# Pooled attention and a GELU layer on one core: k of the later batches turned by a transposing DMA, and four smaller edits

## The chip, the cores and the metric

The kernel runs on one core of one Trainium2 chip. The metric is the device time in microseconds of one execution, as the median of several runs. A profiled execution gives a span (first to last instruction that the hardware profiler saw) and a trace of every engine: TensorE (PE, its weight loads as PEld), VectorE (DVE), ScalarE (ACT), GpSimd (POOL) and SyncE (SP). SP, ACT and POOL also issue DMAs.

## The reference

For each of 8 batches and 8 heads, k and v (576 rows of 64) are averaged over groups of 8 rows, which leaves 72 pooled rows. Then softmax attention of the 576 rows of q against them, and a two-layer network on all 4608 rows:

```python
k_p = k.reshape(B, H, Sp, pool, D).mean(axis=3)       # B=8 H=8 S=576 D=64 pool=8 Sp=72
v_p = v.reshape(B, H, Sp, pool, D).mean(axis=3)
attn = softmax(q @ k_p.T / sqrt(D))
x = (attn @ v_p).transpose(0, 2, 1, 3).reshape(4608, 512)
h = x @ w_in                                           # 512 x 2048
out = gelu_tanh(h) @ w_out                             # 2048 x 512
```

## The kernel before

**Groups.** The order of all instructions is written out by hand. Batch 0's attention is a start of its own. Then nine groups of 512 rows of the network follow (`for g in range(NG)`). A group has two halves. In p1, 64 matmuls of 512 columns (`p1_mm`, 16 tiles `fo` of four steps `ko`) make h, and ACT applies gelu to each tile into `gT`. In p2, 64 matmuls of 512 columns (`p2_mm`, four row blocks `r` of 16 steps) make the output; `store` copies a block from PSUM to one of six buffers `osb` on VectorE, and SP sends it out in four DMAs. Between the p2 matmuls, at the hand-set places `pos`, lies the attention of the next batch `nb = g + 1`: `qk` (scores of two heads), `expo` (exponential on ACT), `av` (attention times v, with the denominator in the unused half of the columns), `norm` and `mult`.

**k and v.** `load_k` brings k of a batch to `kt`, four pooled rows of 2 KB to a partition, head after head, as 128 partitions of 8 KB and a rest of 64 partitions in a fifth slot; the lower 64 partitions of that slot take v's last eight pooled rows of every head. `k_steps` are three additions on VectorE that halve the eight summands each time and leave `kp`. `trans_k_mm` (L173) turns `kp` on TensorE in five transposes, and `trans_k_copy` copies the result from PSUM into two tiles `kT`, six copies each (L183 to L194). Each of the two has 64 of its 128 rows filled and the others zero. For a head in the upper half of the heads, the pooled rows are placed so that rows 64 to 127 come first and eight rows stand at 0 to 7; `pool_rows` says how many rows are used (72 or 128), and `vp`, `vz` and `ones` are laid out alike. `v_steps` adds v's main rows (64 of each head) into `vp`; `v_moves` moves the last eight by two DMAs on SP.

**q.** Batches 0 and 1 are turned on TensorE (L203). From batch 2 on, `load_q` (on POOL, with a cast to bf16) brings q to `qb`, and `trans_q_dma` (L223) turns it by a transposing DMA on SP, which waits for the load.

**Loads ahead.** `load_next` issues, for batch g + 2: the q load on POOL, the q transpose on SP, a tiny copy on POOL (`gate`, L453) that holds POOL until the transpose has landed, and then the k and v loads on POOL. In groups 1 to 5 it stands at the start of the group, in group 0 behind p1. Since POOL has nothing else to do, the q load of a batch is issued right behind the v loads of the batch before.

**What lies beside p1.** The dictionary `plan` says behind which gelu the additions, transposes and copies are emitted: in groups from 1 on, k's additions behind tiles 2 and 3, v's behind 7 and 8, and the five transposes of k behind 9.

**The start.** Batch 0's k and v are loaded first, by SP and ACT. POOL then loads q of batch 0, w_in in two parts, k of batch 1, q of batch 1 and w_out in four parts. v of batch 1 is loaded by SP once VectorE has reached a one-element memset of its tile (L421), which stands after the first `mult0`. In group 0 p2 takes w_out quarter by quarter.

**The end.** The last row block of the last group is split by columns into 384 and 128; each part is copied and stored in four DMAs, two on SP and two on ACT.

Of the kernel before, what the change touches and what calls it, by code (L numbers as in the profile page):

```python
# [8 lines left out]
F32 = mybir.dt.float32  # L9
# [9 lines left out]
def kernel(  # L19
# [9 lines left out]
    nc = tc.nc  # L29
# [23 lines left out]
    opool = ctx.enter_context(tc.tile_pool(name="op", bufs=6))  # L53
# [11 lines left out]
    kts = [consts.tile([128, KR + 1, 512], F32, name=f"kt{i}") for i in range(2)]  # L65

    def load_k(b, engs):
        rows = k[b].rearrange("h (j l) d -> (h j) (l d)", l=8)
        main = rows[0:128 * KR].rearrange("(p r) c -> p r c", r=KR)
        n = KR // len(engs)  # L70
        for i, eng in enumerate(engs):
            eng.dma_start(out=kts[b % 2][:, i * n:(i + 1) * n], in_=main[:, i * n:(i + 1) * n])
        engs[0].dma_start(out=kts[b % 2][64:128, KR], in_=rows[128 * KR:])
        rows = v[b].rearrange("h (j l) d -> j h (l d)", l=8)
        for i in range(2):
            engs[-1].dma_start(out=kts[b % 2][32 * i:32 * i + 32, KR], in_=rows[64:, 4 * i:4 * i + 4])  # L76
# [41 lines left out]
    kTs = [[consts.tile([128, H, 128], BF16, name=f"kT{i}{e}") for e in range(2)] for i in range(2)]  # L118
    kps = [consts.tile([128, KR + 2, D], BF16, name=f"kp{i}") for i in range(2)]

    vps = [consts.tile([128, H, 2, D], BF16, name=f"vp{i}") for i in range(2)]

    vz = consts.tile([128, H, 2, D], BF16, name="vz")
    ones = consts.tile([128, 2, 3, D], BF16, name="ones")
# [6 lines left out]
    for half, j0, j1 in ((0, 0, 128), (1, 0, 8), (1, 64, 128)):  # L131
        nc.vector.memset(ones[j0:j1, half, 1], 8.0)
# [4 lines left out]
    def add(o, a, b):  # L137
        nc.vector.tensor_tensor(out=o, in0=a, in1=b, op=ALU.add)  # L138
# [8 lines left out]

    def v_moves(b):

        for i in range(2):  # L150
            nc.sync.dma_start(out=vps[b % 2][64 - 64 * i:72 - 64 * i, 4 * i:4 * i + 4, 0],
                              in_=kps[b % 2][32 * i:32 * i + 32, KR])

    def v_steps(b):
        t = vts[b % 2]
        w = (vps[b % 2] if b else vz)[:, :, 0]

        def main():
            for i in range(2):
                p = slice(64 * i, 64 * i + 64)  # L160
                add(w[p, 4 * i:4 * i + 4], t[p, :, 0:64], t[p, :, 64:128])

        return [lambda: add(t[:, :, 0:256], t[:, :, 0:256], t[:, :, 256:512]),
                lambda: add(t[:, :, 0:128], t[:, :, 0:128], t[:, :, 128:256]), main]
# [10 lines left out]
    def trans_k_copy(b, e, bank, lower=True, upper=True):  # L175


        tp = half_bank(bank)[0:D, 0:(KR + 1) * 128].rearrange("p (r c) -> p r c", c=128)
        o = kTs[b % 2][e][e * 64:(e + 1) * 64]
        copy = nc.vector.tensor_copy  # L180

        def heads(h0, h1, c0, j0, j1):
            copy(out=o[:, h0:h1, c0:c0 + (j1 - j0) * KR].rearrange("p h (j r) -> p h j r", r=KR),  # L183
                 in_=tp[:, 0:KR, h0 * KH:h1 * KH].rearrange("p r (h j) -> p h j r", j=KH)[:, :, j0:j1])

        if lower:
            heads(0, 4, 0, 0, KH)
        if upper:
            heads(4, H - 1, 64, 0, 16)
            heads(4, H - 1, 0, 16, KH)  # L190
            copy(out=o[:, H - 1, 64:72].rearrange("p (j r) -> p j r", r=KR),
                 in_=tp[:, 0:KR, (H - 1) * KH:128].rearrange("p r j -> p j r"))
            copy(out=o[:, H - 1, 72:128], in_=tp[:, KR, 64:120])
            copy(out=o[:, H - 1, 0:8], in_=tp[:, KR, 120:128])  # L194
# [36 lines left out]
    def pool_rows(pr):  # L231
        return Sp if pr < PR // 2 else 128

    def qk(b, c, pr, bank):
        for e in range(2):
            h = 2 * pr + e
            n = pool_rows(pr)
            nc.tensor.matmul(out=PS[:n, bank + e, :CH].rearrange("j (t p) -> j t p", p=32),  # L238
                             lhsT=kTs[b % 2][c][:, h, :n],
                             rhs=qTs[b][:, h // 4, :, h % 4 * 32:h % 4 * 32 + 32],  # L240
                             start=True, stop=True)

    def expo(b, c, pr, bank):
        n = pool_rows(pr)
        e = ep.tile([128, 2, CH], BF16, name="e", bufs=8)
        nc.scalar.activation(out=e[:n], in_=PS[:n, bank:bank + 2, :CH], func=ACT.Exp, scale=1.0 / 64.0)  # L246
        es[b, c, pr] = e
# [6 lines left out]
    def av(b, c, pr, bank):  # L254


        e = es.pop((b, c, pr))
        n = pool_rows(pr)
        for x in range(2):
            nc.tensor.matmul(out=PS[:, bank + x, :CH], lhsT=window(vps[b % 2][:n], 2 * pr + x),  # L260
                             rhs=e[:n, x, :], start=True, stop=True)
# [20 lines left out]
    def den0(c, pr, bank):  # L282
        for x in range(2):
            e = es[0, c, pr + x]
            n = pool_rows(pr)
            for y in range(2):
                one = ones[:n, pr // 2].rearrange("j a d -> j (a d)")[:, 64 - 64 * y:192 - 64 * y]
                nc.tensor.matmul(out=PS[:, bank + x, :CH], lhsT=one, rhs=e[:n, y, :],
                                 start=(y == 0), stop=(y == 1))
# [8 lines left out]
    def av0(c, pr, bank):  # L298
        for x in range(2):
            e = es.pop((0, c, pr + x))  # L300
            n = pool_rows(pr)
            for y in range(2):
                nc.tensor.matmul(out=PS[:, bank + x, :CH], lhsT=window(vz[:n], 2 * (pr + x) + y),
                                 rhs=e[:n, y, :], start=(y == 0), stop=(y == 1))
# [22 lines left out]
    def o_bank(g, r):  # L327
        return 1 - x_bank(g) if r % 2 == 0 else x_bank(g)
# [3 lines left out]
    def p1_mm(g, fo, ko, c0=0, c1=GROUP):  # L332
        r0 = g * GROUP
        q, j = divmod(fo % 8, 4)
        nc.tensor.matmul(out=PS[:, h_bank(g, fo), c0:c1], lhsT=w_in_b[fo // 8][:, ko, q * 512 + j:(q + 1) * 512:4],  # L335
                         rhs=xT[:, ko, r0 + c0:r0 + c1], start=(ko == 0), stop=(ko == KO - 1))

    def gelu(g, fo):
        if g not in gTs:
            gTs[g] = gpool.tile([128, FO, GROUP], BF16, name="gT")  # L340
        nc.scalar.activation(out=gTs[g][:, fo, :], in_=PS[:, h_bank(g, fo), :], func=ACT.Gelu_apprx_tanh)  # L341
# [5 lines left out]
    osbs = {}  # L347

    def store(g, r, bank, c0=0, c1=DM):
        if (g, r) not in osbs:  # L350
            osbs[g, r] = opool.tile([128, DM], F32, name="osb")
        osb = osbs[g, r]
        nc.vector.tensor_copy(out=osb[:, c0:c1], in_=PS[:, bank, c0:c1])  # L353

        for n in range(4):
            b, col = divmod(g * GROUP + r * 128 + n * 32, S)
            rows = out[b * S:(b + 1) * S].rearrange("(p t e) d -> e t p d", t=TP, e=2)
            eng = nc.scalar if c1 - c0 < DM and n % 2 else nc.sync
            eng.dma_start(out=rows[col // CH, col % CH // 32, :, c0:c1], in_=osb[n * 32:(n + 1) * 32, c0:c1])
# [30 lines left out]
    for h in range(H):  # L390
        i = h // 4
        nc.tensor.matmul(out=PS[64 - 64 * i:72 - 64 * i, 7, h * D:(h + 1) * D],
                         lhsT=identb[0:64, 32 * i + h % 4:32 * i + 32:4], rhs=kps[0][0:64, KR],
                         start=True, stop=True)
# [3 lines left out]
    for i in range(2):  # L398
        p = slice(64 - 64 * i, 72 - 64 * i)
        nc.vector.tensor_copy(out=vz[p, 4 * i:4 * i + 4, 0],  # L400
                              in_=PS[p, 7, 256 * i:256 * i + 256].rearrange("p (h d) -> p h d", d=D))
# [18 lines left out]

    nc.vector.memset(vts[1][:, 0, 0:1], 0.0)  # L421
    load_v(1, [nc.sync])
# [12 lines left out]
    nc.vector.memset(kTs[1][1], 0.0)  # L435
    for w in vps:
        nc.vector.memset(w, 8.0)
        nc.vector.memset(w[0:64, H // 2:], 0.0)
        nc.vector.memset(w[0:8, H // 2:], 8.0)
# [5 lines left out]
    for g in range(NG):  # L445
# [3 lines left out]
        def load_next():  # L449

            load_q(g + 2)
            trans_q_dma(g + 2)
            nc.gpsimd.tensor_copy(out=gate, in_=qTs[g + 2][0:1, 1, TP - 1, 0:2])  # L453
            load_k(g + 2, [nc.gpsimd])
            load_v(g + 2, [nc.gpsimd])

        if 0 < g and g + 2 < B:
            load_next()
# [3 lines left out]
        if nb is not None:  # L462
            kk = k_steps(nb)
# [3 lines left out]
            if g:  # L467
# [64 lines left out]
    for c0, c1, bank in ((0, 384, o_bank(g, 3)), (384, DM, 4)):  # L532
        for fo in range(FO):
            p2_mm(g, 3, fo, bank, c0, c1)
        store(g, 3, bank, c0, c1)
# [30 lines left out]
```

The softmax here doesn't subtract the row's maximum and nothing guards it: scores larger than these inputs give would overflow.

## Time and profile before

| | |
|---|---|
| median of 3 runs | 307.75 us (306.88 to 308.21) |
| profiled execution | 307.9 us, span 306.1 us |
| TensorE busy | 296.8 us, 97% of the span |
| ScalarE, VectorE, GpSimd busy | 219.0, 150.5, 35.0 us |
| granted TensorE clock | full in every part of the span |
| DMA | 41.12 MB, 134 GB/s on average; nearly full until 45 us, about half full until 215 us, little after |
| software queue q0 (POOL) | 33.7% of 16 engines |
| hardware queue q1 (SP) | 21.1% |

The page gives busy time by engine, the chain of waits that ended last, the costliest groups of instructions with the idle time ahead of them, and the DMA issues with their time to landing. A busy TensorE is an average over stages: what an edit is worth is read in its own stage. Times in the timelines count from the span's start.

### The profile page before, as it was taken

What the parts mean: (1) busy time and instruction counts of PE and PEld (TensorE: products, weight loads), DVE (VectorE), ACT (ScalarE), POOL (GpSimd) and SP (SyncE); (2) the same over time, 40 slices, a digit from 0 to 9 for tenths busy, and PEclk for the clock granted to TensorE, in tenths of its full rate; (3) what the DMA queues carried; (4) which work ended last, traced back from release to release, by engine and by line L of the source; (5) the groups of instructions that cost most, each with busy time, mean ns of one, the idle gap of its engine ahead of it and who ended that gap; (6) DMA issues with size and microseconds to landing.
All of it is one profiled execution on the core that took longest, in us unless ns stands there. A gap on an engine that the chain in (4) does not pass through costs nothing.

```text
span 306.1 us, 4354 instructions
## 1 busy us (share of the span) xinstructions
PE 296.8 (97%) x1528; PEld 157.6 (51%) x1557; DVE 150.5 (49%) x336; ACT 219.0 (72%) x402; POOL 35.0 (11%) x67
## 2 busy tenths in 40 slices
PE   8999899999999999999999999999999999999994
PEld 3555455555555555555555555555555555445543
DVE  5885757572577057805682559245932630120012
ACT  1687489867987798779977898789868986206500
POOL 7102002305003200320014000400000000000000
PEclk9999999999999999999999999999999999999999
DMA  7999987977955962696159827672101210121022
GB/s 221 266 254 264 227 171 139 310 168 184 257 138 113 278 154 53 118 279 154 35 112 250 181 61 103 203 153 71 35 1 36 59 44 0 36 70 35 2 68 69
DMA packets 30806, 41.12 MB, mean 134 GB/s; under 512 B 18176, under 2 KB 18432, under 8 KB 29888
## 3 DMA queue, kind: packets, MB, share of 16 engines
q0 software_dynamic: 7568, 24.38, 33.7%
q1 hardware_dynamic: 22528, 15.14, 21.1%
q10 hardware_dynamic: 688, 1.31, 1.3%
q8 instruction: 12, 0.20, 0.3%
q14 instruction: 10, 0.08, 0.1%
HBM read 36.70 MB, written 9.44 MB: 151 GB/s over the span
## 4 chain that ended last, share of the span: by engine, by line
PE 87%; DMA 11%; issue 1%; ACT 0%; DVE 0%; POOLq 0%
PE PS L344 40%; PE PS L335 37%; DMA qb<-in_q_dram 11%; PE PS L238 5%; PE PS L260 4%; PE PS L173 1%; PE PS L203 0%; ACT e L246 0%; ACT ld L268 0%; ACT ld L267 0%; DVE osb L353 0%; POOLq L550 0%
## 5 line engine op out<-in xcount | busy, mean ns | idle before, releaser
L344 PE MATMUL PS<-w_out_b,gT 128*128 128x512 bf16 (+2 forms) x577 | 133.9, 373 | 0.7
L335 PE MATMUL PS<-xT,w_in_b 128*128 128x512 bf16 x563 | 126.6, 379 | 0.7
L341 ACT ACTIVATE gT<-PS 128x512 bf16<-128x512 f32 x144 | 81.2, 603 | 48.1 <-PE PS L335 48.0
L335 PEld LDWEIGHTS <-w_in_b 128*128 128x128 bf16 x576 | 64.7, 113 | 57.2
L344 PEld LDWEIGHTS <-gT 128*128 128x128 bf16 x592 | 57.0, 97 | 55.7 <-issue 0.4
L353 DVE COPY osb<-PS 128x512 f32<-128x512 f32 (+2 forms) x37 | 25.1, 677 | 98.2 <-PE PS L344 78.6
L278 DVE TENSOR_TENSOR xT<-PS,rc 64x288 bf16<-64x288 f32 x112 | 50.9, 455 | 31.7 <-ACT rc L270 27.5
L246 ACT ACTIVATE e<-PS 72x576 bf16<-72x576 f32 (+1 forms) x64 | 41.0, 647 | 8.8 <-PE PS L238 7.9
L238 PE MATMUL PS<-qT,kT 128*72 128x288 bf16 (+1 forms) x128 | 25.8, 286 | 0.9 <-ACT qT L213 0.6
L270 ACT ACTIVATE rc<-ld 128x288 f32<-128x288 f32 x56 | 24.8, 444 | 1.8
L313 ACT ACT_TABLE_LOAD x17 | 21.8, 1283 | 4.3 <-issue 4.1
L267 ACT ACTIVATE ld<-PS 64x288 f32<-64x288 f32 x56 | 22.8, 408 | 1.3
L268 ACT ACTIVATE ld<-PS 64x288 f32<-64x288 f32 x56 | 22.5, 402 | 1.4
L260 PE MATMUL PS<-e,vp 72*128 72x288 bf16 (+1 forms) x112 | 23.1, 286 | 0.0
L138 DVE TENSOR_TENSOR kt<-kt 128x1280 f32<-128x1280 f32 (+5 forms) x18 | 18.9, 1048 | 7.6 <-DMA kt<-in_v_dram 4.6
L238 PEld LDWEIGHTS <-kT 128*72 128x72 bf16 (+1 forms) x128 | 13.2, 105 | 15.1 <-DVE qT L215 1.2
L453 POOL COPY gate<-qT 1x2 bf16<-1x2 bf16 x6 | 1.0, 174 | 138.5 <-DMA qT<-qb 138.5
L138 DVE TENSOR_TENSOR vt<-vt 128x1024 f32<-128x1024 f32 (+1 forms) x16 | 15.3, 956 | 1.7 <-DMA vt<-in_v_dram 1.4
L183 DVE COPY kT<-PS 64x288 bf16<-64x288 bf16 (+2 forms) x48 | 13.0, 318 | 6.2 <-PE PS L173 6.0
L260 PEld LDWEIGHTS <-vp 72*128 72x128 bf16 (+1 forms) x112 | 11.0, 98 | 3.8
L365 PE MATMUL PS<-idle 128*128 128x512 bf16 x32 | 10.4, 468 | 1.6 <-DVE idle L126 1.2
L76 POOL DMA_DIRECT2D kt<-in_v_dram x14 | 8.0, 586 | 0.1
(48 smaller groups left out, 88.8 us busy)
## 6 DMA issues: line engine op xcount, KB each, us to landing
out_dram<-osb SPq DMA_DIRECT2D x140, 64.0 KB
kt<-in_k_dram POOLq DMA_DIRECT2D x7, 1024.0 KB, 6.0
vt<-in_v_dram POOLq DMA_DIRECT2D x12, 512.0 KB, 8.7
qb<-in_q_dram POOLq DMA_DIRECT2D x7, 576.0 KB, 11.8
w_in_b<-in_moe_w_in_dram POOLq DMA_DIRECT2D x2, 1024.0 KB, 16.8
w_out_b<-in_moe_w_out_dram POOLq DMA_DIRECT2D x4, 512.0 KB, 19.3
vt<-in_v_dram SPq DMA_DIRECT2D x3, 512.0 KB
kt<-in_k_dram POOLq DMA_DIRECT2D x7, 128.0 KB, 6.0
```

What stands on the lines that cost most here:

```text
L138: nc.vector.tensor_tensor(out=o, in0=a, in1=b, op=ALU.add)
L238: nc.tensor.matmul(out=PS[:n, bank + e, :CH].rearrange("j (t p) -> j t p", p=32), lhsT=kTs[b % 2][c][:, h, :n], rhs=qTs[b][:, h // 4, :, h ...
L246: nc.scalar.activation(out=e[:n], in_=PS[:n, bank:bank + 2, :CH], func=ACT.Exp, scale=1.0 / 64.0)
L260: nc.tensor.matmul(out=PS[:, bank + x, :CH], lhsT=window(vps[b % 2][:n], 2 * pr + x), rhs=e[:n, x, :], start=True, stop=True)
L267: nc.scalar.activation(out=ld[0:64], in_=PS[64:128, bank, :CH], func=ACT.Ln)
L268: nc.scalar.activation(out=ld[64:128], in_=PS[0:64, bank + 1, :CH], func=ACT.Ln)
L270: nc.scalar.activation(out=rc, in_=ld, func=ACT.Exp, scale=-1.0)
L278: nc.vector.tensor_tensor(out=xT[rows, pr, col:col + CH], in0=PS[rows, bank + x, :CH], in1=rc[rows], op=ALU.mult)
L335: nc.tensor.matmul(out=PS[:, h_bank(g, fo), c0:c1], lhsT=w_in_b[fo // 8][:, ko, q * 512 + j:(q + 1) * 512:4], rhs=xT[:, ko, r0 + c0:r0 + c ...
L341: nc.scalar.activation(out=gTs[g][:, fo, :], in_=PS[:, h_bank(g, fo), :], func=ACT.Gelu_apprx_tanh)
L344: nc.tensor.matmul(out=PS[:, bank, c0:c1], lhsT=gTs[g][:, fo, r * 128:(r + 1) * 128], rhs=w_out_b[:, fo, c0:c1], start=(fo == 0), stop=(fo ...
L353: nc.vector.tensor_copy(out=osb[:, c0:c1], in_=PS[:, bank, c0:c1])
```

## The change

k of batches 0 to 2 is turned on TensorE as before. From batch 3 on (`KX = 3`), `load_k_dma` loads k with the pooled row as the partition (72 partitions, eight pieces of 2 KB in each, one per head) and v's last rows into partitions 96 to 127 of the same tile; `k_steps_dma` adds on VectorE, writes the pooled k twice into a zeroed tile `kz` (the second time by a copy), and has SP turn that by a transposing DMA into `kx`, a tile of 16 blocks, which `qk` reads. k's steps stand behind the first gelu of the group, and `load_next` behind them; a second tiny copy on POOL holds the loads of the next batch until `kx` has landed. For all batches the pooled rows of a head now stand at 0 to 71 (`pool_rows` is gone), the second half of v's main rows is written from partitions 64 to 127 to partitions 0 to 63, v's last rows take one load and one move (two for batches from 3 on), and `trans_k_copy` has four copies instead of six. The memset that lets v of batch 1 be loaded stands behind the memsets of `kT`. In the last group, gelu writes the columns of each row block in another order, so that 32 rows that were together lie four partitions apart; the last block is split into 256 and 256 columns, each stored by one DMA, the first on ACT and the last on SP. There are five output buffers instead of six.

```diff
-    opool = ctx.enter_context(tc.tile_pool(name="op", bufs=6))
+    opool = ctx.enter_context(tc.tile_pool(name="op", bufs=5))
...
-    kts = [consts.tile([128, KR + 1, 512], F32, name=f"kt{i}") for i in range(2)]
+    kts = [consts.tile([128, H, 512], F32, name=f"kt{i}") for i in range(2)]
+    KX = 3
...
-        for i in range(2):
-            engs[-1].dma_start(out=kts[b % 2][32 * i:32 * i + 32, KR], in_=rows[64:, 4 * i:4 * i + 4])
+        engs[-1].dma_start(out=kts[b % 2][0:64, KR], in_=rows[64:])
+
+    def load_k_dma(b):
+        nc.gpsimd.dma_start(out=kts[b % 2][0:Sp], in_=k[b].rearrange("h (j l) d -> j h (l d)", l=8))
+        rows = v[b].rearrange("h (j l) d -> j h (l d)", l=8)
+        for y in range(2):
+            nc.gpsimd.dma_start(out=kts[b % 2][96:128, y], in_=rows[64 + 4 * y:68 + 4 * y])
...
+    def k_steps_dma(b):
+        t = kts[b % 2]
+        k0, k1 = (kz[0:Sp, :, e, e * D:e * D + D] for e in range(2))
+        m, x = t[0:Sp], t[96:128, 0:2]
+        return [lambda: add(m[:, :, 0:256], m[:, :, 0:256], m[:, :, 256:512]),
+                lambda: add(m[:, :, 0:128], m[:, :, 0:128], m[:, :, 128:256]),
+                lambda: add(k0, m[:, :, 0:64], m[:, :, 64:128]),
+                lambda: nc.vector.tensor_copy(out=k1, in_=k0),
+                lambda: trans_k_dma(b),
+                lambda: add(x[:, :, 0:256], x[:, :, 0:256], x[:, :, 256:512]),
+                lambda: add(x[:, :, 0:128], x[:, :, 0:128], x[:, :, 128:256]),
+                lambda: add(kps[b % 2][96:128, 0:2], x[:, :, 0:64], x[:, :, 64:128])]
+
+    kxs = {}
+
+    def trans_k_dma(b):
+        kxs[b] = bp.tile([128, 2 * H, 128], BF16, name="kx")
+        nc.sync.dma_start_transpose(out=kxs[b], in_=kz.rearrange("p h e c -> p (h e c)"))
+
     def v_moves(b):
 
-        for i in range(2):
-            nc.sync.dma_start(out=vps[b % 2][64 - 64 * i:72 - 64 * i, 4 * i:4 * i + 4, 0],
-                              in_=kps[b % 2][32 * i:32 * i + 32, KR])
+        if b >= KX:
+            for y in range(2):
+                nc.sync.dma_start(out=vps[b % 2][64 + 4 * y:68 + 4 * y, :, 0], in_=kps[b % 2][96:128, y])
+            return
+        nc.sync.dma_start(out=vps[b % 2][64:Sp, :, 0], in_=kps[b % 2][0:64, KR])
...
-                add(w[p, 4 * i:4 * i + 4], t[p, :, 0:64], t[p, :, 64:128])
+                add(w[0:64, 4 * i:4 * i + 4], t[p, :, 0:64], t[p, :, 64:128])
...
-            heads(4, H - 1, 64, 0, 16)
-            heads(4, H - 1, 0, 16, KH)
-            copy(out=o[:, H - 1, 64:72].rearrange("p (j r) -> p j r", r=KR),
-                 in_=tp[:, 0:KR, (H - 1) * KH:128].rearrange("p r j -> p j r"))
-            copy(out=o[:, H - 1, 72:128], in_=tp[:, KR, 64:120])
-            copy(out=o[:, H - 1, 0:8], in_=tp[:, KR, 120:128])
+            heads(4, H - 1, Sp, 4 * KH, 7 * KH)
+            heads(H - 1, H, 8, 7 * KH, 128)
+            nc.vector.tensor_copy(out=o[:, H - 1, 8:Sp], in_=tp[:, KR, 64:128])
...
-                             lhsT=kTs[b % 2][c][:, h, :n],
+                             lhsT=kxs[b][:, 2 * h + c, 0:Sp] if b >= KX else kTs[b % 2][c][:, h],
...
-        nc.scalar.activation(out=gTs[g][:, fo, :], in_=PS[:, h_bank(g, fo), :], func=ACT.Gelu_apprx_tanh)
+        o, i = gTs[g][:, fo, :], PS[:, h_bank(g, fo), :]
+        if g + 1 == NG:
+
+            o, i = o.rearrange("f (r p t) -> f r t p", r=4, t=4), i.rearrange("f (r t p) -> f r t p", r=4, t=4)
+        nc.scalar.activation(out=o, in_=i, func=ACT.Gelu_apprx_tanh)
...
-            eng.dma_start(out=rows[col // CH, col % CH // 32, :, c0:c1], in_=osb[n * 32:(n + 1) * 32, c0:c1])
+            nc.sync.dma_start(out=rows[col // CH, col % CH // 32],
+                              in_=osb[n::4] if g + 1 == NG else osb[n * 32:(n + 1) * 32])
...
     mult0(0, 0, 4)
-
-    nc.vector.memset(vts[1][:, 0, 0:1], 0.0)
-    load_v(1, [nc.sync])
     den0(1, 2, 6)
...
     nc.vector.memset(kTs[1][1], 0.0)
+
+    nc.vector.memset(vts[1][:, 0, 0:1], 0.0)
+    load_v(1, [nc.sync])
     for w in vps:
         nc.vector.memset(w, 8.0)
-        nc.vector.memset(w[0:64, H // 2:], 0.0)
-        nc.vector.memset(w[0:8, H // 2:], 8.0)
+    nc.gpsimd.memset(kz, 0.0)
...
+            if nb >= KX:
+                nc.gpsimd.tensor_copy(out=gate, in_=kxs[nb][0:1, 2 * H - 1, 0:2])
             load_q(g + 2)
             trans_q_dma(g + 2)
             nc.gpsimd.tensor_copy(out=gate, in_=qTs[g + 2][0:1, 1, TP - 1, 0:2])
-            load_k(g + 2, [nc.gpsimd])
+            if g + 2 >= KX:
+                load_k_dma(g + 2)
+            else:
+                load_k(g + 2, [nc.gpsimd])
             load_v(g + 2, [nc.gpsimd])
 
-        if 0 < g and g + 2 < B:
+        if 0 < g and nb is not None and nb < KX:
             load_next()
...
-            kk = k_steps(nb)
+            kk = k_steps(nb) if nb < KX else k_steps_dma(nb)
...
-            if g:
+            if nb >= KX:
+                plan = {0: kk + ([load_next] if g + 2 < B else []), 7: vv[:1], 8: vv[1:]}
+            elif g:
                 plan = {2: kk[:1], 3: kk[1:], 7: vv[:1], 8: vv[1:], 9: tk}
...
-    for c0, c1, bank in ((0, 384, o_bank(g, 3)), (384, DM, 4)):
+    for c0, bank in ((0, o_bank(g, 3)), (256, 4)):
+        c1 = c0 + 256
         for fo in range(FO):
             p2_mm(g, 3, fo, bank, c0, c1)
-        store(g, 3, bank, c0, c1)
+        osb = opool.tile([128, 256], F32, name="osb")
+        nc.vector.tensor_copy(out=osb, in_=PS[:, bank, c0:c1])
...
+        (nc.sync if c0 else nc.scalar).dma_start(out=rows[col // CH, :, t:t + 4, c0:c1],
+                                                 in_=osb)
```

## The prediction, made before the changed kernel ran

> **What bounds the kernel now.** I read the busy times first, then the chain of waits, then the groups of instructions, then the timelines of one middle group, of the start and of the end.
>
> ```profile
> PE 296.8 (97%) x1528; PEld 157.6 (51%) x1557; DVE 150.5 (49%) x336; ACT 219.0 (72%) x402; POOL 35.0 (11%) x67
> PE 87%; DMA 11%; issue 1%; ACT 0%; DVE 0%; POOLq 0%
> ```
>
> TensorE is busy for 97% of the span and 87% of the chain that ended last; the 11% of DMA is one piece at the start, a q load from 8.79 us to 33.7 us. So only TensorE time, the start and the tail can move the end, unless the change makes TensorE wait. What TensorE spends on the transposes of k stands in the groups and in its timeline in group 4 (about 151.3 to 183.1 us):
>
> ```profile
> L173 PE MATMUL PS<-identb,kp 128*128 128x128 bf16 x35 | 3.1, 219 | 0.0
> L203 PE MATMUL PS<-identb,qb 128*128 128x128 bf16 x36 | 3.0, 220 | 1.4 <-DMA qb<-in_q_dram 1.4
> ...
> 159.77 0.44 PE L173 MATMUL PS<-identb,kp 128*128 128x128 bf16 x5
> 160.05 5.34 PE L335 MATMUL PS<-xT,w_in_b 128*128 128x512 bf16 x23
> ```
>
> Read the starts, not the durations, because matmuls are pipelined: the five transposes of a batch begin at 159.77 and the next p1 matmul at 160.05, so they take 0.28 us of TensorE. Row L203 shows the one DMA wait of TensorE: 1.4 us at 33.73, for q of batch 1. The rest of the group has no hole: 128 matmuls of 0.216 us, 32 of 0.122 us and 0.28 us make 31.8 us, the distance between groups (119.3, 151.2, 183.0).
>
> Now the loads of that group, on SP, POOL and VectorE:
>
> ```profile
> 154.49 2.77 SPq L223 DMA_TRANSPOSE qT<-qb  x1
> ...
> 159.18 0.17 POOL L453 COPY gate<-qT 1x2 bf16<-1x2 bf16 x1 [27.04 <-DMA qT<-qb]
> 159.72 0.58 POOL L72 DMA_DIRECT2D kt<-in_k_dram  x1 [0.36 <-issue]
> ...
> 163.19 0.76 POOL L86 DMA_DIRECT2D qb<-in_q_dram  x1
> ...
> 153.57 2.35 DVE L138 TENSOR_TENSOR kt<-kt 128x1280 f32<-128x1280 f32 x2
> ...
> kt<-in_k_dram POOLq DMA_DIRECT2D x7, 1024.0 KB, 6.0
> vt<-in_v_dram POOLq DMA_DIRECT2D x12, 512.0 KB, 8.7
> qb<-in_q_dram POOLq DMA_DIRECT2D x7, 576.0 KB, 11.8
> ```
>
> A q transpose takes 4.7 us from issue to the gate (154.49 to 159.18). k lands about 165.7 and isn't added before the next group, about 185: 20 us of slack. q is loaded a group ahead. This slack is what the change spends.
>
> **What the Trainium skill says.** "TensorE: Matmul & The Clock Gate", section "Wait — 56ns, not 53.3ns?", gives 55.6 ns from start to start for 128 columns and 215.7 ns for 512: the trace agrees (0.28 / 5 = 56 ns; 0.216 us). "VectorE: DVE Perf Modes", section on the TRN2 errata, prices an fp32 add of N elements at (N+151)/0.96 ns: the trace has 1226 ns for 1024 elements against 1224. "DMA: Bandwidth & Descriptors", section "Issuing engines are not separate DMA queues", says that all queues share 16 engines: agreed, between 23 and 33 us q1 and q0 divide them. The same page, "Why a DMA increments its semaphore by 16 and not by 1", says that the outermost size sets how many engines a transfer uses: a 72-partition load would get 12, or 15 with 5 partitions each. No transfer here shows that.
>
> **Part 1, k of batches 3 to 7 by DMA.** Removed: 5 x 5 transposes on TensorE, 5 x 0.28 = **1.4 us** on the path, and 12 copies a batch on VectorE (about 2 us in p1, off the path). Added on VectorE, ahead of the first scores: adds of 2048, 1024 and 512 elements, 2.29 + 1.23 + 0.69 us (the first by the formula, the others are rows of v), and a copy of 512 that I put at 0.3 us, bounded by 0.15 and 0.55 (a 512-element copy from PSUM took 0.69): 4.5 us. They run in group 4's place from T = 153.5, when VectorE has finished the group before. Small adds of v's last rows take 1.0 us more. VectorE's p1 work becomes 8.3 us against 7.7 and ends at about T+8.3, before its next job at T+16 (169.62): no cost.
>
> SP then issues the k transpose, 16 blocks against 18 for q: 4.7 x 16/18 = 4.2, say 4.5 us. k is turned at **T+9**. The first scores stand at 166.52 = T+13. Margin 4 us. Behind that instruction on SP wait two 4 KB moves of v, the q transpose and the group's stores. The moves end by T+10.5, needed at T+15. The q transpose now waits for a q load that POOL, held by its new gate, issues only at T+9.6; alone it needs what q takes behind v (first packet after 1.2 us, data 3.5 us, end 1.9 us): 6.6 us. So it lands at T+16, and the stores, due at T+17, start at T+19; four stores take 2.6 us and come every 4.4 us, so SP catches up, with five buffers to spare.
>
> The new **loop** is the crux: k turned, q loaded, q turned, next k loaded, added, turned. Its length: 0.3 (gate) + 6.8 (q, with its issue) + 4.7 + 0.5 + k load + 4.5 + 4.5. The k load now has 2 KB pieces in 72 partitions. v, with 2 KB pieces on 64 partitions, moved 0.2 MB per us; 1.18 MB at that rate is 6 us, at 12/16 of it 7.5; with 2.3 us of ends 8.5 to 10 us, against 6.0 now. Loop: 29.8 to 31.3 us, against a TensorE group of 31.5. It just fits; k lands at the group's start, v 5 us later, still 1 us before VectorE asks. Cost taken: **0**, from 0 to several us.
>
> **Part 2, the start.** Batch 1's v starts loading after the kT memsets, about 22.8 us instead of 18.9. It held the engines together with k and q of batch 1 between 23 and 33 us, at some 37% of them. q of batch 1 gets up to 1.4 us more of the engines before v begins, and lands near 32.4 instead of 33.7: the wait of 1.41 us goes. What is late next: the four w_out quarters, which land at 36.1, 38.5, 41.1 and 43.5 (issue times plus landings), since the total load is the same. TensorE asks for the last at 44.0, so the gain is capped at about 0.5 us. v of batch 1 lands near 37 to 38.5; its 2.8 us of adds now begin at 38.56 and its first use is at 41.12, with 0.2 us to spare. I take **0.4 us**, between -1.0 and +1.4. The memset of kz on POOL (some 2 us) only delays the q load of batch 2, which queues behind w_out until 43.5 anyway: 0. Fewer and smaller memsets and copies at the start save some 0.3 us ahead of the same DMA wait: 0.
>
> **Part 3, the end.**
>
> ```profile
> 301.84 1.80 ACTq L359 DMA_DIRECT2D out_dram<-osb  x4
> 302.15 0.29 DVE L353 COPY osb<-PS 128x128 f32<-128x128 f32 x1 [0.34 <-PE PS L344]
> ```
>
> Columns 384 + 128 become 256 + 256: on TensorE 3.63 becomes 32 x 0.109 = 3.49 us, -0.14; the last copy grows from 0.29 to about 0.43 (between 0.29 and 0.56), +0.14. Then one DMA in place of two on each queue: the last issue ends at 303.05 instead of 303.6; the transfer is 128 KB instead of 16 KB pieces, +0.1 to +0.4. Gain **0.3 us**, between 0 and 0.8. The last group's gelu writes with a stride of four elements; it takes 603 ns and has 866 ns (four matmuls) per tile, so up to 40% more is covered; I take 0. The 512-column stores of that group read every fourth partition: same bytes, 0. Five output buffers against six: 0, since a copy waits for the store five before it, some 20 us old.
>
> **Sum.** 1.4 + 0.4 + 0.3 = 2.1 us. The profiled execution took 307.9 us around its span of 306.1; it becomes 305.8. That is 0.15 above the median of 307.75, so I say **305.7 us**, own range 304.2 to 306.8 from the bounds of parts 2 and 3. Half a per cent, about what a measurement can tell, is 1.54 us.
>
> **Rivals.** *The loop outruns the group* (slower). Place: the k load of batches 4 to 7. If the load gets 12 engines and transposes and q loads are each 1 us slower beside v and stores, the loop is 34.3 us: each group is 2.8 us later, 11 us over four, less the margin of 4: TensorE waits 7 us at the first scores, and the time is 312.7. It costs anything from a loop of 32.5 on, and the kernel is slower by over 0.5% from about 33.4. For it: slack falls from 20 us to nearly none. Against: my sum of rows stays below 31.5. Chance 0.2 from there on, and some more with a shorter loop that only eats the gain. *The start gives back* (no change): v of batch 1 comes 1 us late, or w_out holds TensorE, the tail gives nothing: or the loop takes 1 to 3 us: 306.4 to 309, chance 0.22. *The start was worth more*: w_out comes earlier too and the whole 1.4 us stays: 304.7, chance 0.15, inside the faster case. A gelu above 866 ns would cost 13 times the excess, a few per cent of chance, in the slower case. That the change doesn't do what it says is unlikely: in the built program the transposes are gone from TensorE, whose order is otherwise the same in the later groups.
>
> **Chances.** Faster 0.58, the same 0.22, slower 0.20. The range 304.2 to 310.0 leaves out the longer loops (0.15) and a little below (0.04).
>
> **What would show it.** The transposes of k on TensorE number 15 instead of 40; the k transposes land about 9 us after VectorE starts on a group, before the first scores, which have no idle time ahead of them; the 1.4 us ahead of the transposes of batch 1's q are gone; the last store is one issue, and the span ends about 2.8 us after it starts. I am wrong if score matmuls of groups 3 to 6 wait for kx, with waits that grow from group to group (the loop), if the first av of group 0 waits for vp, or if ACT's gelu of the last group holds TensorE.

## The result, and the profile after

The changed kernel takes **319.36 us** (median of 4 runs, 318.85 to 319.81), against 307.52 us for the kernel before beside it: ratio 1.0384, 95% interval 1.0354 to 1.0414. It is 11.8 us slower; the forecast was 2.1 us faster, with a range to 310.0. The profiled execution took 319.7 us around a span of 317.9 us, so it stands for the median.

Busy times and the chain of waits that ended last, on the page of the changed kernel:

```profile
PE 298.9 (94%) x1503; PEld 157.8 (50%) x1532; DVE 152.6 (48%) x277; ACT 228.4 (72%) x402; POOL 35.8 (11%) x65
PE 47%; DMA 35%; ACT 7%; DVE 7%; issue 2%; SPq 0%; POOL 0%; POOLq 0%; DVEq 0%; ACTq 0%
```

TensorE had 87% of the chain before and has 47% now; DMA has gone from 11% to 35%, ACT from nothing to 7%. ACT's busy time is 9.4 us longer with the same 402 instructions: some of them must have become slower. To see where, I set the start of each group's p1 (its first matmul with w_in) side by side:

| us from the span's start | before | after | difference of the stretch |
|---|---|---|---|
| group 1 begins | 55.6 | 58.3 | **+2.7** |
| groups 1 to 3, to the start of group 4 | 151.1 | 153.3 | -0.5 |
| groups 4 to 6, to the start of group 7 | 246.7 | 254.2 | **+5.4** |
| group 7, to the start of group 8 | 274.3 | 281.8 | 0 |
| p1 of group 8 ends | 288.1 | 300.0 | **+4.4** |
| end | 306.1 | 317.9 | -0.1 |

Three stretches lose, by three different waits. The waits of TensorE, in the view that adds them by what they waited for (us in total, times, longest), of the changed kernel:

```profile
PE PS L257 <- DMA kx<-kz: 5.6, 3, 2.1
PE PS L277 <- DVE vp L146: 2.5, 1, 2.5
PE PS L351 <- ACT gT L361: 1.3, 1, 1.3
```

The wait of 1.4 us for q of batch 1 is not among them any more. In its place are one for v of batch 1 (`vp`), three for `kx`, and one for gelu, whose 1.3 us is too small for its stretch; the experiments settle that.

**The loop.** One turn of it, in the timelines of SP, POOL and VectorE of the changed kernel:

```profile
131.59 2.01 SPq L173 DMA_TRANSPOSE kx<-kz  x1
142.16 3.37 SPq L246 DMA_TRANSPOSE qT<-qb  x1
166.01 1.77 SPq L173 DMA_TRANSPOSE kx<-kz  x1
...
136.03 0.17 POOL L462 COPY gate<-kx 1x2 bf16<-1x2 bf16 x1 [19.59 <-DMA kx<-kz]
136.49 0.73 POOL L93 DMA_DIRECT2D qb<-in_q_dram  x1 [0.28 <-issue]
148.00 0.17 POOL L465 COPY gate<-qT 1x2 bf16<-1x2 bf16 x1 [10.79 <-DMA qT<-qb]
148.60 0.88 POOL L80 DMA_DIRECT2D kt<-in_k_dram  x1 [0.43 <-issue]
...
161.35 3.54 DVE L146 TENSOR_TENSOR kt<-kt 72x2048 f32<-72x2048 f32 x2 [5.66 <-DMA kt<-in_k_dram]
```

From one k transpose (131.59) to the next (166.01) are 34.4 us: 4.9 to the q load, 11.5 for q to be loaded and turned, 0.6 to the k load, **12.75** from its issue to the first add, 4.7 for the adds. The k transposes are issued at 97.31, 131.59, 166.01, 199.90 and 233.37, every 33.5 to 34.4 us, where a group of TensorE takes 31.6. So the first scores of groups 4, 5 and 6 wait, as the timeline of TensorE shows for the first two (idle time ahead in brackets):

```profile
170.31 0.44 PE L257 MATMUL PS<-qT,kx 128*72 128x288 bf16 x2 [1.73 <-DMA kx<-kz]
204.18 0.44 PE L257 MATMUL PS<-qT,kx 128*72 128x288 bf16 x2 [2.10 <-DMA kx<-kz]
```

Each turn adds what it is longer than a group, some 2 us. The single waits stay near that size (1.7, 2.1 and 1.7 us), because each of them also moves the next group back; it is their sum that grows. Four turns take 136.1 us and four groups 126.3; of the 9.7 us between them 5.6 are waits, and the rest was slack of the first turns.

The DMA issues of the changed kernel give the loads (KB each, median us from issue to landing):

```profile
kt<-in_k_dram POOLq DMA_DIRECT2D x5, 1152.0 KB, 12.7
qb<-in_q_dram POOLq DMA_DIRECT2D x7, 576.0 KB, 6.5
```

k took 6.0 us before. q, which now starts when it is wanted and not a group ahead, takes 6.5 instead of 11.8.

**The start.** Timelines of TensorE and VectorE, and below them windows at and behind the wait (from:to, length, then busy time and instructions of PE, PEld, DVE, ACT, POOL; granted TensorE clock; DMA share; GB/s), of the changed kernel:

```profile
36.12 1.46 PE L364 MATMUL PS<-w_out_b,gT 128*128 128x512 bf16 x6
42.27 0.64 PE L277 MATMUL PS<-e,vp 72*128 72x288 bf16 x2 [2.47 <-DVE vp L146]
...
39.79 1.95 DVE L146 TENSOR_TENSOR vt<-vt 128x1024 f32<-128x1024 f32 x2 [2.88 <-DMA vt<-in_v_dram]
```

```profile
38.60:42.01 3.41, 1.20 (x7) 0.45 (x5) 2.15 (x3) 0.70 (x2) 0.00 (x0) 1.00 1.09 209
42.01:45.42 3.41, 2.93 (x8) 1.35 (x10) 1.51 (x4) 1.25 (x3) 0.00 (x0) 0.50 0.47 91
45.43:45.60 0.17, 0.17 (x4) 0.12 (x3) 0.00 (x0) 0.00 (x0) 0.00 (x0) 1.00 0.00 0
```

The first w_out matmul now starts at 36.1 and not at 37.6: the q wait is gone, a gain of 1.5 us. But v lands only when VectorE starts on it at 39.79, the first av waits 2.47 us, and then something comes that no list of waits contains: for 3.41 us TensorE runs at a clock of 0.50. What that costs shows in the time from this av to the start of group 1: 16.0 us here, 14.5 us in the kernel before, and 14.5 us again in a kernel below that has the same wait and keeps its full clock. That is 1.5 us. -1.5 + 2.5 + 1.5 = 2.5 us, nearly all of the stretch's +2.7.

**The last group.** Gelu, as the view of its source line lists it (count, then nanoseconds least/median/most, starts of the first and the last), for its strided form in the changed kernel:

```profile
L361 ACT ACTIVATE gT<-PS x16: 1327/1416/1423, 284.9 to 301.9; 128x512 bf16<-128x512 f32 x16
```

### The profile page after: what moved, and what is told of

Read it like the earlier page. It is cut to its first block, busy times and chain, and to the rows that moved or that the text cites. A ratio compares the mean times of both kernels' runs of the same rounds, so it can differ in the third digit from the quotient of the medians.

```text
span 317.9 us, 4254 instructions
## 1 busy us (share of the span) xinstructions
PE 298.9 (94%) x1503; PEld 157.8 (50%) x1532; DVE 152.6 (48%) x277; ACT 228.4 (72%) x402; POOL 35.8 (11%) x65
## 4 chain that ended last, share of the span: by engine, by line
PE 47%; DMA 35%; ACT 7%; DVE 7%; issue 2%; SPq 0%; POOL 0%; POOLq 0%; DVEq 0%; ACTq 0%
PE PS L364 26%; PE PS L351 14%; DMA kt<-in_k_dram 12%; DMA qb<-in_q_dram 6%; DMA kx<-kz 5%; DMA vt<-in_v_dram 5%; ACT gT L361 5%; DMA qT<-qb 5%; PE PS L257 3%; DVE kt L146 3%; PE PS L277 3%; DMA out_dram<-osb 2%; ACT e L264 1%; DVE kz L146 1%; ACT rc L311 1%
## 5 line engine op out<-in xcount | busy, mean ns | idle before, releaser
L364 PE MATMUL PS<-w_out_b,gT 128*128 128x512 bf16 (+1 forms) x575 | 135.6, 375 | 1.1 <-issue 0.2
L361 ACT ACTIVATE gT<-PS 128x512 bf16<-128x512 f32 x144 | 90.6, 693 | 42.7 <-PE PS L351 42.7
L369 DVE COPY osb<-PS 128x512 f32<-128x512 f32 x35 | 24.2, 692 | 88.3 <-PE PS L364 88.1
L264 ACT ACTIVATE e<-PS 72x576 bf16<-72x576 f32 x64 | 40.9, 645 | 16.9 <-PE PS L257 16.1
L146 DVE TENSOR_TENSOR kt<-kt 72x2048 f32<-72x2048 f32 (+9 forms) x28 | 30.4, 1084 | 27.1 <-DMA kt<-in_k_dram 23.4
L277 PE MATMUL PS<-e,vp 72*128 72x288 bf16 x112 | 23.3, 288 | 2.5 <-DVE vp L146 2.5
L284 ACT ACTIVATE ld<-PS 64x288 f32<-64x288 f32 x56 | 22.8, 408 | 3.5 <-PE PS L277 2.2
L257 PE MATMUL PS<-qT,kx 128*72 128x288 bf16 x80 | 16.4, 287 | 5.7 <-DMA kx<-kz 5.6
L257 PEld LDWEIGHTS <-kx 128*72 128x72 bf16 x80 | 8.8, 113 | 15.2 <-DMA kx<-kz 7.0
L277 PEld LDWEIGHTS <-vp 72*128 72x128 bf16 x112 | 11.0, 99 | 6.0 <-DVE vp L146 2.7
L257 PE MATMUL PS<-qT,kT 128*72 128x288 bf16 x48 | 9.6, 288 | 0.9 <-ACT qT L236 0.6
## 6 DMA issues: line engine op xcount, KB each, us to landing
vt<-in_v_dram POOLq DMA_DIRECT2D x12, 512.0 KB, 14.5
kt<-in_k_dram POOLq DMA_DIRECT2D x5, 1152.0 KB, 12.7
```

The source lines that it names most:

```text
L257: nc.tensor.matmul(out=PS[:Sp, bank + e, :CH].rearrange("j (t p) -> j t p", p=32), lhsT=kxs[b][:, 2 * h + c, 0:Sp] if b >= KX else kTs[b % ...
L264: nc.scalar.activation(out=e, in_=PS[:Sp, bank:bank + 2, :CH], func=ACT.Exp, scale=1.0 / 64.0)
L284: nc.scalar.activation(out=ld[0:64], in_=PS[64:128, bank, :CH], func=ACT.Ln)
L361: nc.scalar.activation(out=o, in_=i, func=ACT.Gelu_apprx_tanh)
L364: nc.tensor.matmul(out=PS[:, bank, c0:c1], lhsT=gTs[g][:, fo, r * 128:(r + 1) * 128], rhs=w_out_b[:, fo, c0:c1], start=(fo == 0), stop=(fo ...
L369: nc.vector.tensor_copy(out=osb, in_=PS[:, bank])
```

## The experiments

The theory after the result had three independent parts: the loop through POOL's gate is longer than a group, because of the k load; v of batch 1 comes too late; the strided gelu holds TensorE. Each has its rivals: that the scores wait for the new adds and the transpose themselves, that v's place only chooses which load is late, that the last p1 waits for something other than gelu. All experiments start from the changed kernel. Ratios are to the kernel before, with 95% intervals.

**Put v's load back where it was**, behind the first `mult0`.

```diff
     mult0(0, 0, 4)
+    nc.vector.memset(vts[1][:, 0, 0:1], 0.0)
+    load_v(1, [nc.sync])
...
     nc.vector.memset(kTs[1][1], 0.0)
-    nc.vector.memset(vts[1][:, 0, 0:1], 0.0)
-    load_v(1, [nc.sync])
```

> The changed kernel with one edit undone: the load of batch 1's v is let go where it was before, after the first mult0. Theory: the late v costs the start 2.7 us net. In the changed kernel p2 of group 0 begins 1.5 us earlier than before (36.1 against 37.6 us), but TensorE then waits 2.5 us for vp, after which its granted clock is 0.50 to 0.64 until 46 us, and group 1 begins at 58.4 instead of 55.7. Undone, the 1.4 us wait for q of batch 1 comes back, the wait for vp and the low clock go: group 1 begins at 55.6 to 55.9, time 316.3 to 317.0. Rival (the start gives back nothing, DMA is simply full until 45 us): group 1 still begins after 57.5 and the time stays at 319.

Measured: 317.36 us (315.69 to 319.27), ratio 1.0312 (1.0249 to 1.0376): 2.0 us less than the changed kernel in the median, with a wide spread. The profiled execution took 318.7 us. It has group 1 at 58.2, as late as the changed kernel, because the wait had only moved. Timeline and window of TensorE of this kernel:

```profile
34.68 0.72 PE L226 MATMUL PS<-identb,qb 128*128 128x128 bf16 x5 [2.37 <-DMA qb<-in_q_dram]
```

```profile
34.70:36.50 1.80, 1.58 (x8) 0.97 (x10) 0.49 (x1) 0.00 (x0) 0.00 (x0) 0.50 1.09 218
```

q of batch 1 is 2.37 us late instead of v, and again the clock falls to half behind the gap. The kernel before waits for the same q 1.41 us, and its clock stays full. Why q is a microsecond later here than in the kernel before, with v's load in the same place, is open. It isn't the same in every execution: two kernels below have this same start, and their profiles show q 0.97 and 2.54 us late. What divides the four runs into 315.7 and 316.0 on one side and 318.7 and 319.3 on the other is open too: each pair has one run with a mean clock of 1.000 and one with 0.994 or 0.995. So this experiment alone doesn't show what v's place costs.

**Let gelu write contiguously** and read PSUM in the permuted order instead, so the same values go to places that p2 reads in the same way; the first line only permutes.

```diff
-            o, i = o.rearrange("f (r p t) -> f r t p", r=4, t=4), i.rearrange("f (r t p) -> f r t p", r=4, t=4)
+            o, i = o.rearrange("f (r p t) -> f r p t", r=4, t=4), i.rearrange("f (r t p) -> f r p t", r=4, t=4)
```

> The changed kernel with one edit: in the last group gelu reads PSUM in the permuted order and writes gT contiguously, in place of reading in order and writing with a step of four elements; the result has the same layout. Theory: the write with a step is what takes gelu from 603 to about 1158 ns, and TensorE, which makes a tile in 866 ns, waits for it (p1 of the last group 18.0 us against 13.7): with contiguous writes gelu takes about 603 to 650 ns, p1 13.7 us, time 315.0 to 315.4. Rival: any permuted access costs ScalarE the same, gelu stays above 1.1 us and the time at 319; or the read costs and gelu lies between.

Measured: 314.27 us, ratio 1.0221 (1.0192 to 1.0250). p1 of the last group takes 13.8 us (281.5 to 295.3) as before the change, instead of 18.2. The source line of gelu in this kernel:

```profile
L361 ACT ACTIVATE gT<-PS x16: 592/597/645, 284.6 to 295.5; 128x512 bf16<-128x512 f32 x16
```

597 ns, the median of the gelus of the kernel before. So the stride on the SBUF write is what costs, and the permuted read from PSUM costs nothing. In the changed kernel a gelu takes about 1.42 us, but the next one starts before it ends, 1.14 us after it (284.9 to 301.9 us in 15 steps). TensorE makes a tile in 0.87 us; 16 x 0.27 = 4.3 us, against the stretch's 4.4. The view of waits had put only 1.3 us of this down to gelu, because TensorE counts as busy for most of the delay: 15.7 us of the 18.2 between 281.8 and 300.0, for 64 matmuls that take 13.8 us here. The starts of the stages show it, the list of waits doesn't.

**Take the new gate away**, so that POOL issues the next loads without waiting for `kx`.

```diff
-            if nb >= KX:
-                nc.gpsimd.tensor_copy(out=gate, in_=kxs[nb][0:1, 2 * H - 1, 0:2])
             load_q(g + 2)
```

> The changed kernel without the second tiny copy on POOL, the one that waits for kx: the q load of the next batch is issued right behind the v load of the one before, as before the change. Theory: the loop (k turned, q loaded, q turned, k loaded, added, turned; 33.5 to 34.4 us from kx to kx against 31.5 of TensorE) is what makes TensorE wait for kx in groups 4 to 6. Without the q load in it the loop is about 27 us, k lands before the group begins, TensorE does not wait, groups 2 to 6 are 31.5 us each: 313.0 to 314.0. Rival: the k load itself (12.7 us) or SP's order is the bound, kx stays late and the time is above 317.

Measured: 313.74 us, ratio 1.0195 (1.0157 to 1.0233). No wait for `kx` is left, and groups 1 to 6 take 31.6 us each on average (58.5 to 248.2). The transposes and the adds are all still there, which excludes the rivals for this stretch: it is the loop. k still takes 11.9 us to land, now with a whole group to do it in.

**Turn all k on TensorE**, with `load_next` at the start of groups from 1 on.

```diff
-    KX = 3
+    KX = B
...
-        if 0 < g and nb is not None and nb < KX:
+        if 0 < g and g + 2 < B:
             load_next()
```

> The changed kernel with k of all batches turned on TensorE (KX = 8), and load_next at the group's start for groups 1 to 5 as before the change; everything else as changed. Theory: part 1 costs 4.8 us net, groups 1 to 6 take 195.9 us in the changed kernel and 191.0 before: 314.3 to 315.0. Rival: the groups are longer for another reason (later group 0, five output buffers, v's layout), then they stay near 195 us and the time above 317.

Measured: 314.25 us, ratio 1.0223 (1.0186 to 1.0261). No `kx` exists, no loop, and groups of 31.8 us (58.5 to 249.6), as in the kernel before. Against 31.6 us in the kernel without the gate, the five transposes are worth 0.27 us a batch.

**Split the k load** at 64 partitions, with the gate in place.

```diff
-        nc.gpsimd.dma_start(out=kts[b % 2][0:Sp], in_=k[b].rearrange("h (j l) d -> j h (l d)", l=8))
+        krows = k[b].rearrange("h (j l) d -> j h (l d)", l=8)
+        nc.gpsimd.dma_start(out=kts[b % 2][0:64], in_=krows[0:64])
+        nc.gpsimd.dma_start(out=kts[b % 2][64:Sp], in_=krows[64:Sp])
```

> The changed kernel with the k load of batches 3 to 7 cut in two: 64 partitions in one DMA, the other 8 in a second; the waiting copy on POOL stays. Theory: the 72-partition load lands only after 12.7 us because it uses fewer of the 16 engines (12 of them would carry 48 pieces of 2 KB each, about 7.9 us at v's rate, plus some 2.3 us of ends and the stores that now run beside it). With 64 partitions it lands after 9.5 to 10.5 us, the loop is 31 to 32 us, the waits for kx in groups 4 to 6 (5.6 us) all but go: 313.5 to 315. Rival: the 2 KB pieces and the stores beside them set the pace; k still lands after 12 us or more and the time stays above 318.

Measured: 313.02 us, ratio 1.0179 (1.0157 to 1.0201). The DMA issues of this kernel:

```profile
kt<-in_k_dram POOLq DMA_DIRECT2D x7, 1024.0 KB, 8.5
kt<-in_k_dram POOLq DMA_DIRECT2D x7, 128.0 KB, 10.1
```

The second is issued 0.7 us after the first, so k is complete about 10.8 us after its first issue instead of 12.7. The k transposes start every 31.2 to 31.9 us, the loop no longer outruns the group, no `kx` wait is left, and groups take 31.6 us. Only the shape of one load differs: with this gate, its 72 partitions in one piece are what made the loop too long.

TensorE waits for `vp` here too, 2.62 us, but in this profile the clock stays at 1.00, and from the av to group 1 are 14.5 us (42.8 to 57.3) instead of 16.0. Two of this kernel's four runs have a mean clock of 1.000 and took 312.4 and 312.5 us, two have 0.994 to 0.995 and took 313.5 and 313.6. One stretch of 3.41 us at half clock takes 0.005 off the mean of a run of this length. The last section shows on what it depends.

**All three causes at once**: v early, gelu read permuted, no gate.

> The changed kernel with three edits undone or replaced: v of batch 1 let go after the first mult0, gelu of the last group reading the permuted order and writing contiguously, no waiting copy for kx on POOL. Theory (the three causes add up): e2 and e3 took away 5.1 and 5.6 us from 319.4, which leaves 308.7 with the late v; the early v trades the wait for vp for one for q of batch 1, of 1.4 to 2.4 us; where that wait stays under some 2.1 us the clock keeps full and the time is 306 to 307, where it is longer the clock halves for about 4 us and it is 308.5 to 309.5. Rival: the causes overlap, the time stays above 310.

Measured: 307.00 us, ratio 0.9993 (0.9984 to 1.0002). The three account for the whole loss: alone the edits gain 2.0, 5.1 and 5.6 us, 12.7 together, and all at once 12.4. Two waits are seen that the forecast of 305.7 did not have. TensorE still waits 1.0 us for q of batch 1. And in group 1, where `load_next` still stands ahead of k's steps, SP's queue holds v's move behind the q transpose of batch 3. Timelines of SP and TensorE of this kernel:

```profile
68.94 2.71 SPq L246 DMA_TRANSPOSE qT<-qb  x1
71.76 0.67 SPq L181 DMA_DIRECT2D vp<-kp  x1
...
73.91 0.42 PE L277 MATMUL PS<-e,vp 72*128 72x288 bf16 x2 [0.75 <-DMA vp<-kp]
```

**v of batch 1 on POOL's queue**, right behind q of batch 1 and in place of the load on SP, with the gelu and gate edits; and the same with the k load split.

```diff
+    load_v(1, [nc.gpsimd])
...
-    nc.vector.memset(vts[1][:, 0, 0:1], 0.0)
-    load_v(1, [nc.sync])
```

> As the run before it (gelu reads permuted, no waiting copy for kx), but v of batch 1 is loaded by POOL, in its queue right behind q of batch 1 and ahead of w_out. Theory: what the start lost is the order of transfers on engines that are full until 45 us, v behind w_out's quarters. In one queue q of batch 1 lands before 32 us and v about 4 us behind it, so TensorE waits for neither, the clock stays full, p2 of group 0 starts at 36.1 and group 1 at 54.2 to 54.9: 304.5 to 305.5, below the kernel before. Rival: w_out's quarters, pushed behind v, now hold TensorE in group 0 (group 1 starts at 56 or later): 306.5 or more.

> As the run before it with the k load cut into 64 and 8 partitions as well. Theory: without the waiting copy the loop has slack, so an earlier k brings nothing: within 0.5 us of the run before it. Rival: the load's end still touches the group (x rows, v), then it is 1 us or more faster.

Measured: 309.29 us, ratio 1.0066 (1.0049 to 1.0082), and 308.94 us, 1.0065 (1.0037 to 1.0093). At the start neither q nor v is waited for beyond 0.2 us, but w_out queues behind v now, and in group 1 of the first of the two v's move is 1.1 us late, as it was 0.75 us late in the kernel above. TensorE of the first of the two waits 1.0 us for w_out, in two pieces:

```profile
37.04 1.47 PE L365 MATMUL PS<-w_out_b,gT 128*128 128x512 bf16 x6 [0.48 <-DMA w_out_b<-in_moe_w_out_dram]
39.73 1.46 PE L365 MATMUL PS<-w_out_b,gT 128*128 128x512 bf16 x6 [0.54 <-DMA w_out_b<-in_moe_w_out_dram]
```

In the second it waits 2.9 us for w_out. Up to 45 us the engines are full: a load that is moved ahead makes another late.

**Mend group 1 as well**: the three edits, the split, and `load_next` of group 1 behind k's steps; first with v early, then with v's load in a place between the two, behind `mult0(0, 2, 4)` (issued at 20.8 us; early is 19.0 in the kernel before, late 22.8).

```diff
-        if 0 < g and nb is not None and nb < KX:
-            load_next()
...
-                plan = {2: kk[:1], 3: kk[1:], 7: vv[:1], 8: vv[1:], 9: tk}
+                plan = {2: kk[:1], 3: kk[1:] + [load_next], 7: vv[:1], 8: vv[1:], 9: tk}
```

> The three edits of e6 (early v of batch 1, gelu reading permuted, no waiting copy for kx), the k load cut into 64 and 8 partitions, and in group 1 load_next behind k's steps, so that the move of v's last rows of batch 2 on SP is issued ahead of the q transpose of batch 3, which waits for its load. Theory: in e6 group 1 was 32.8 us because TensorE waited 0.8 us for that move (SP held until 68.9 us); it goes, group 1 is 31.9 us again, and with the 1.4 us of transposes the time is 306.0 to 306.5, 0.3% below the kernel before. Rival: k of batch 3 comes later for it, or the start varies by more than that: 306.8 or more.

> As the run before it, with v of batch 1 let go one place later, after the first mult0 of the upper heads (about 20.7 us; early is 18.9, the changed kernel 22.8). Theory: in the start q of batch 1 and v of batch 1 share full DMA engines, and each is late where the other is early; between the two places q's wait is under 0.7 us and v lands before 37.5 us, so neither holds TensorE for long: group 1 starts at 54.5 to 55.2 and the time is 305.3 to 306.0. Rival: the sum is fixed and the two waits only trade, with group 1 at 55.4 or later and no gain over the run before it.

Measured with v early: 308.79 us, ratio 0.9993 (0.9960 to 1.0026; ratios are of means, and the kernel before has a median of 308.16 us here). Two of six executions, with a mean clock of 1.000, took 306.7 and 307.0 us; the four with 0.994 took 308.6 to 309.1. The profile is one of these four and shows q of batch 1 2.54 us late:

```profile
34.77 0.68 PE L228 MATMUL PS<-identb,qb 128*128 128x128 bf16 x5 [2.54 <-DMA qb<-in_q_dram]
```

With v in the middle: **306.42 us, ratio 0.9934 (0.9907 to 0.9962)**, two thirds of a per cent below the kernel before. All six executions have a mean clock of 0.997 or more. Against the two of v early with full clock it is only 0.3 to 0.6 us faster, so most of what the middle place gives is that none of its executions has the lower mean clock. TensorE at the start of this one:

```profile
33.13 0.45 PE L228 MATMUL PS<-identb,qb 128*128 128x128 bf16 x5 [0.69 <-DMA qb<-in_q_dram]
...
40.53 0.41 PE L279 MATMUL PS<-e,vp 72*128 72x288 bf16 x2
```

q waits 0.69 us, v not at all, the clock stays full to 56 us, and group 1 begins at 55.1. It still loses 1.5 us in group 1, where the transposes of k wait 1.3 us for VectorE's `kp`, and VectorE had waited 4.8 us for the load of that batch.

## Why the prediction was wrong, by its own steps

**Part 1, cost of the loop taken as 0: the step that failed first of all**, in the stretch that lost 5.4 of the 11.8 us. The chain of steps was right, and all terms but one, the k load:

| term | forecast | measured |
|---|---|---|
| k turned, gate, q load issued | 4.8 | 4.9 |
| q loaded and turned | 11.5 | 11.5 |
| to the k load's issue | 0.5 | 0.6 |
| k load to the first add | 8.5 to 10 | **12.75** |
| adds and copy | 4.5 | 4.7 |
| sum | 29.8 to 31.3 | 34.4 |

The k load was priced from v's rate, 0.2 MB per us on 64 partitions, with 12/16 of it for 72 partitions. Both rates were too high. As an estimate, with the same 2.3 us for the two ends, 64 partitions with these pieces moved 1.05 MB in 8.5 - 2.3 = 6.2 us, 0.17 MB per us, and 72 moved 1.18 MB in 12.7 - 2.3 = 10.4 us, 0.113: two thirds, where 12/16 had been assumed. The prediction drew on the Trainium skill, "DMA: Bandwidth & Descriptors", section "Why a DMA increments its semaphore by 16 and not by 1", for 12 engines. The experiment agrees in direction, since the 64-partition load is much faster. That engines stand idle in the 72-partition one is not shown: in the changed kernel, from 153.0 to 161.4 us, while k lands, the mean share of the 16 engines is 1.00 to 1.07, with v's loads and stores beside it. So the shape of the load is shown as the cause, and why this shape is slow stays open.

The rival named this place, the k load of batches 4 to 7, a loop of 34.3 us and 7 us of waits, and got a chance of 0.2. The runs gave 33.5 to 34.4 and 5.6 us, and the margin of 4 us before the first wait came out as 4.1. One of its signs was wrong in form: the single waits do not grow from group to group. A step whose slack fell from 20 us to between 0.2 and 1.7, on a load of a shape no row showed, deserved more than that.

**Part 1, gain of 1.4 us: right.** Transposes on TensorE number 15; groups without the loop's waits are 31.6 us against 31.8, 0.27 us for each of five. That VectorE would have room was right too.

**Part 2, +0.4 gain with v "0.2 us to spare": failed.** The q wait went, as said. v began at 22.8, as assumed, but landed at 39.7 instead of 37 to 38.5: from 27 to 37 us its packets had 22 to 29% of the engines and not the 37% of the kernel before. The wait of 2.5 us lies where the prediction named its own refutation (the first av of group 0), but its price was put at 1.0 at most. The half clock behind it, 1.5 us, was in none of the cases. The cap by w_out was not reached in this kernel; moving v ahead of w_out, as on POOL's queue, reached it.

**Part 3, gelu's stride at 0: failed.** "Up to 40% more is covered" was the right test with no price in it: the stride cost 137% (597 to 1416 ns). The rival, "13 times the excess", has the right form; with 1.14 us from start to start against 0.87 it is 16 tiles and 4.3 us. The tail itself gave 0.1 us in the changed kernel and 0.3 with all three causes undone, against 0.3.

**The sum.** With the three steps mended, the middle place of v and group 1's order, the time is 0.66% below the kernel before, 2.0 us, close to the 2.1 of the forecast; but part of that comes from edits that the forecast knew nothing of, so the agreement is in part luck and does not confirm the sum term by term.

## What to carry to other kernels

When an edit spends slack, compare what is left with the uncertainty of the term that no row shows; a margin of 0.2 to 1.7 us against a load priced by analogy is none. In a stretch where the DMA engines are full, moving one load only chooses which consumer waits, so look for the place where all of them just make it. Put a permutation on the side of an instruction where it costs nothing: here reading PSUM with a stride was free, and writing bf16 to SBUF with one more than doubled the time of an instruction. A wait of two or three microseconds can also cost clock behind it, in some executions and not in others, so take several runs before explaining a difference of 1.5 us.

## What the runs showed of the hardware

- ScalarE, 128x512 from fp32 in PSUM to bf16 in SBUF: 597 ns contiguous or with the read permuted, 1416 ns when it writes every fourth element.
- A load into 72 partitions (eight pieces of 2 KB each) took 12.7 us, into 64 and 8 as two loads about 10.8, of which the first 8.5.

**A short hole in TensorE's work can cost twice, and whether it does depends on where it falls.** In all twelve traces the granted clock changes only at whole steps of 3.41 us. In the changed kernel it rises at 4.47 us (the 512-column matmuls then start every 0.22 us instead of every 0.43), falls at 42.01, which is 11 steps later, and rises again at 45.43. The clock of a step follows what TensorE did in the step before it:

| kernel | gap of TensorE, us | TensorE busy in the step of 3.41 us that holds most of it | clock in the step behind |
|---|---|---|---|
| no gate | 2.56 | 0.79 | 0.50 |
| all three, group 1 mended, v early | 2.54 | 0.88 | 0.50 |
| all k on TensorE | 2.52 | 0.93 | 0.50 |
| v early | 2.37 | 1.06 | 0.50 |
| the changed kernel | 2.47 | 1.20 | 0.50 |
| gelu reading permuted | 2.21 | 1.20 | 0.50 |
| v on POOL, k load split | 2.64 | 1.45 | 1.00 |
| k load split | 2.62 | 1.66 | 1.00 |

The last two rows as windows, with the step of the kernel with v on POOL first, then that of the kernel with the split load and the step behind it:

```profile
35.01:38.42 3.41, 1.45 (x14) 0.85 (x12) 3.11 (x10) 2.48 (x3) 0.00 (x0) 1.00 1.07 199
...
41.04:44.45 3.41, 1.66 (x10) 0.93 (x10) 1.97 (x5) 1.25 (x3) 0.00 (x0) 1.00 0.80 153
44.45:47.87 3.42, 3.42 (x21) 1.88 (x19) 1.53 (x3) 2.95 (x6) 0.00 (x0) 1.00 0.32 63
```

The half clock came where TensorE was busy for at most 1.20 us of the 3.41, and never where it was busy for 1.45 us or more; what happens between the two was not seen. The longest gaps did no harm because the edge of a step cut them in two, so a limit on the gap alone, such as the 2.1 us of one expectation above, does not hold. The edges lie elsewhere in each execution (the first rise is at 4.47 us in the changed kernel and at 6.91 in the one with the split load), so the same wait can cost 1.5 us more in one execution than in the next. The Trainium skill, "TensorE: Matmul & The Clock Gate", section "What's actually happening", tells of a free-running activity window of 3.4 us, with which these traces agree. Its advice in "Why this matters for your kernels", no idle gaps above about 3 us, was not strict enough here: 2.21 us were enough where they fell into one step. The mean clock of a run doesn't tell its time by itself: two of the sixteen runs with all three edits have 0.993 and took 306.8 and 307.0 us, no longer than the others.
